# Second MLP's w_in operands at five steps a unit, and its first x operands in two halves

## The chip, the core and the metric

The kernel runs on one core of a Trainium2 chip. The metric is the device time of one execution in microseconds (us); smaller is better. Five engines work side by side, each through its own queue in order: PE (TensorE, matmuls), ACT (ScalarE), DVE (VectorE), POOL (GpSimd) and SP (SyncE, which here issues nearly all DMAs).

## What is computed

Linear attention, then an MLP with a squared ReLU, then an MLP with the Mish activation, all in float32. Cut to what matters:

```python
q_s = softmax(q, axis=-1);  k_s = softmax(k, axis=2)         # (4, 8, 576, 64) each
kv = np.einsum('bhsd,bhse->bhde', k_s, v)
x = np.einsum('bhsd,bhde->bhse', q_s, kv)                    # as (2304 tokens, 512)
h = x @ w_in;   y = (s * np.maximum(h, 0)**2 + b) @ w_out    # 512 -> 2048 -> 512
h = y @ w_in2;  g = h * np.tanh(softplus(h));  out = g @ w_out2
```

## The kernel before

A float32 product is made of three passes of matmuls over two float32r parts of each operand, high and low: `hi` is a cast on ACT, `lo` a subtraction on DVE (`split`, L177).

The first MLP runs in 80 steps: five chunks of tokens (512, 256, 512, 512, 512) by 16 slices f of d_ff. In step n PE does the 12 matmuls of h for step n + 2 (`LEAD`) and the 12 of y for step n; relu, square and `gh` on ACT and `gl` on DVE make y's operands from h. y is summed over the 16 steps of a chunk in four PSUM banks, one for each of the four m. In the last step of a chunk (15, 31, 47, 63, 79) `y_out` (L237) takes the banks out, two on ACT and two on DVE, into four tiles `ys`, and stores each to `y_dram`. The next chunk's y needs the banks.

Beside this the second MLP's weights are prepared in eight units for w_in and eight for w_out. A unit has four steps of work. `prep_load` (L255) makes four tiles, raw r0 and r1, t and s, and loads the raws. `prep_bits` (L262) writes t from the raws on ACT (L268) and DVE. `prep_sums` (L290) writes four sums of blocks of t into s, on DVE, and casts t into r0 and s into r1 on ACT. `prep_out` (L307) takes the casts off t and s and stores all four tiles to DRAM (`wi_d`, `wo_d`). `at(step, what, ...)` (L587) puts such work into a list for a step, and the main loop (L743) runs the lists: "prep" and "load" after `y_out`.

The tiles of a unit and the `ys` of `y_out` come from the same pool, "convert" (`cv`, L69), tag "t", four slots. From step 61 (`END`) on there is a second such pool, "convert2" (`cv2`), in the space that attention leaves. A tile has its slot from its first write until its last reader is done.

The order of an engine's instructions is not the program's alone. The framework lists them by a timeline of its own: what comes earlier in the program goes first, but an instruction further back goes ahead while those before it wait. So a load or a bit operation can run some steps before the step in which it is written.

At step 72 (`NS - 8`) the pool "second_x" opens, and `x_load` loads the first 768 tokens of y back as four tiles xf and adds a bias on ACT (L723); at step 74 `x_ops` makes from them the seven pairs of x operands `xo` in two halves j, with four tiles t1 to t4 each from a tag "c" with five slots (L735 to L741). At step 77 the pool "second_w" opens and the weights' ring starts to load. After step 79 the second MLP runs (`p` products on PE), with the seven products of a Strassen-like scheme.

The lines on which the prediction leans most:

```python
t1, t2, t3, t4 = (pools["x"].tile([P, HC], F32, tag="c", bufs=5, ...) for n in range(4))
tt(t1, b12, b11, ALU.subtract)
tt(t3, b22, b12, ALU.subtract)
tt(t2, b22, t1, ALU.subtract)
```

```python
        if f == NF - 1:
            y_out(n)
        run(n, "prep")
        run(n, "load")
```

Of the kernel before, what the change touches and what calls it, by code (L numbers as in the profile page):

```python
# [27 lines left out]
def kernel(  # L28
# [26 lines left out]
    NK = DM // P  # L55
# [13 lines left out]
    cv = ctx.enter_context(tc.tile_pool(name="convert", bufs=4))  # L69
# [43 lines left out]
    def load_raw(ph, z, f, part):  # L113
        src = srcs[ph, z].bitcast(I32)
        if z == "wi":
            nc.sync.dma_start(
                out=part.rearrange("p (k f) -> p k f", k=NK),
                in_=src[:, 2 * f * P:2 * (f + 1) * P].rearrange("(k p) f -> p k f", p=P),
            )
        else:  # L120
            nc.sync.dma_start(out=part, in_=src[f * P:(f + 1) * P, :])
# [55 lines left out]
    def split(hi, lo, src):  # L177
        nc.scalar.copy(out=hi, in_=src)  # L178
        minus(nc.vector, lo, src, hi)
# [27 lines left out]
    def emit_h(m, kks=None):  # L207
        ph, c, f = steps[m]
        if m not in h_ps:
            h_ps[m] = ps_h.tile([P, CM], F32, tag="h", name=f"h{m}")[:, 0:CHUNKS[c]]  # L210
        wh, wl = W[ph, "wi", f]
        for kk in kks or range(NK):
            o = slice(kk * P, (kk + 1) * P)
            passes(h_ps[m], (wh[:, o], wl[:, o]), x_t[ph, c, kk], kk == 0, kk == NK - 1)

    def emit_relu2(m):

        n = CHUNKS[steps[m][1]]
        hi = gp.tile([P, CM], F32R, tag="gh", name=f"gh{m}")[:, 0:n]
        lo = gp.tile([P, CM], F32R, tag="gl", name=f"gl{m}")[:, 0:n]  # L220
        r = rp.tile([P, CM], F32, tag="r", name=f"r{m}")[:, 0:n]
        nc.scalar.activation(out=r, in_=h_ps.pop(m), func=AF.Relu)  # L222
        nc.scalar.activation(out=r, in_=r, func=AF.Square)  # L223
        split(hi, lo, r)
        g_t[m] = (hi, lo)

    def emit_y(n):
        ph, c, f = steps[n]
        nt = CHUNKS[c]
        if f == 0:  # L230
            y_ps[c] = [ps_y.tile([P, DM], F32, tag=f"y{m}", name=f"y{m}_{n}") for m in range(NK)]
        wh, wl = W[ph, "wo", f]
        for m in range(NK):
            o = slice(m * P, (m + 1) * P)
            passes(y_ps[c][m][:, 0:nt], (wh[:, o], wl[:, o]), g_t[n], f == 0, f == NF - 1)

    def y_out(n):  # L237
        c = steps[n][1]
        nt = CHUNKS[c]
        for m, ps in enumerate(y_ps.pop(c)):  # L240
            ys = cv.tile([P, 2 * DM], F32, tag="t", name=f"ys{m}_{n}")[:, 0:nt]
            if m % 2:
                nc.vector.tensor_scalar(
                    out=ys, in0=ps[:, 0:nt], scalar1=sb_s, scalar2=None, op0=ALU.mult
                )
            else:
                nc.scalar.activation(out=ys, in_=ps[:, 0:nt], func=AF.Copy, scale=sb_s)
            nc.sync.dma_start(out=y_dram[c][:, m, :], in_=ys)
# [4 lines left out]
    prep = {}  # L253

    def prep_load(z, i, pool):  # L255
        r = [pool.tile([P, 2 * DM], I32, tag="t", name=f"r{j}_{z}{i}") for j in range(2)]
        for j in range(2):
            load_raw(1, z, i + j * NF // 2, r[j])
        t, s = (pool.tile([P, 2 * DM], F32, tag="t", name=f"{a}_{z}{i}") for a in "ts")
        prep[z, i] = (r, t, s)  # L260
# [26 lines left out]
    def tt(out, a, b, op):  # L287
        nc.vector.tensor_tensor(out=out, in0=a, in1=b, op=op)  # L288
# [298 lines left out]
    def at(slot, what, fn, *args):  # L587
        todo.setdefault((slot, what), []).append((fn, args))

    def run(slot, *what):  # L590
        for x in what:
            for fn, args in todo.pop((slot, x), ()):
                fn(*args)

    for c in range(1, NC):
        wide = CHUNKS[c - 1] == CM
        for hp in range(NP):
            s = (c - 1) * NF + 3 * hp - (c > 1)
# [24 lines left out]
    for i in range(NU):  # L623
        u, s = (0, i), i - 3
# [21 lines left out]
    END = (NC - 1) * NF - 3  # L646
    pools = {}
    for i in range(NF // 2):
        s = (17, 24, 31, 35, 39, 43, 47, 51)[i]
        at(s, "load", lambda i: prep_load("wi", i, cv), i)  # L650
        at(s + 1, "prep", prep_bits, "wi", i)
        at(s + 2, "prep", prep_sums, "wi", i)
        at(s + 3, "prep", prep_out, "wi", i)
        s = (55, 59, 62, 63, 66, 67, 70, 71)[i]
        at(s, "load", lambda i: prep_load("wo", i, pools["cv2"] if i in (2, 4, 6) else cv), i)
        at(s + 1, "prep", prep_bits, "wo", i)
        at(s + 2, "prep", prep_sums, "wo", i)
        at(s + 3, "prep", prep_out, "wo", i)
# [33 lines left out]
    def halves(t):  # L692

        n = t.shape[-1] // 2
        return t[:, 0:n], t[:, n:2 * n]
# [4 lines left out]
    def ring():  # L700
        return pools["ring"].tile([P, 2 * DM], F32R, tag="ring", name="ring")

    def wi_load(i):
        w = [ring() for _ in range(4)]
        for piece, t in enumerate(w):
            o = slice(HD if piece == 3 else 0, DM)
            nc.sync.dma_start(
                out=t.rearrange("p (n d) -> p n d", n=2)[:, :, o].bitcast(F32), in_=wi_d[i][:, piece, :, o]
            )
        return w  # L710

    xo = {}

    def x_load(sc):
        xf = []
        for kk in range(NK):
            t = pools["x"].tile([P, 2 * HC], F32, tag="s1", bufs=4, name=f"xf{sc}_{kk}")
            o = 0
            for c, a, b in PARTS[sc]:
                nc.sync.dma_start(out=t[:, o:o + b - a], in_=y_dram[c][:, kk, a:b])  # L720
                o += b - a

            nc.scalar.activation(out=t, in_=t, func=AF.Identity, bias=bsum[:, kk:kk + 1])  # L723
            xf.append(t)
        return xf

    def x_ops(sc, xf):
        for p in range(1, 8):
            xo[p] = halves(pools["x"].tile([P, 4 * HC], F32R, tag=f"xo{p}", name=f"xo{sc}_{p}"))

        for j in range(2):
            o = slice(j * HC, (j + 1) * HC)
            b11, b12 = xf[j][:, 0:HC], xf[j][:, HC:2 * HC]
            b21, b22 = xf[2 + j][:, 0:HC], xf[2 + j][:, HC:2 * HC]
            t1, t2, t3, t4 = (pools["x"].tile([P, HC], F32, tag="c", bufs=5, name=f"t{n}_{sc}") for n in range(4))  # L735
# [3 lines that stand above are left out]
            tt(t4, b21, t2, ALU.subtract)  # L739
            for p, b in ((1, b11), (2, b21), (6, t2), (5, t1), (7, t3), (3, b22), (4, t4)):  # L740
                split(xo[p][0][:, o], xo[p][1][:, o], b)  # L741

    for n in range(NS):  # L743
        ph, c, f = steps[n]
        if n == END:
            att.close()
            pools["cv2"] = ctx.enter_context(
                tc.tile_pool(name="convert2", bufs=4, side="right", reuse_waits="tile")
            )
        if n == NS - 8:  # L750
            wps[0][0].close()
            pools["x"] = ctx.enter_context(tc.tile_pool(name="second_x", bufs=1, side="right", reuse_waits="tile"))
            xf = x_load(0)
        if n == NS - 6:
            x_ops(0, xf)
        if n == NS - 3:
            wps[1][0].close()
            pools["ring"] = ctx.enter_context(tc.tile_pool(name="second_w", bufs=RING, side="right", reuse_waits="tile"))
            wi_next = {i: wi_load(i) for i in range(2)}
        m = n + LEAD  # L760
        boundary = m < NS and steps[m][2] == 0
        run(n, "att5", "att2", "att3")
        if n < NF:
            run(n, "abs", "hi", "lo", "bits")
        run(n, "att4_mm")
        if boundary:
            emit_y(n)
        if m < NS:
            emit_h(m)
            emit_relu2(m)  # L770
        run(n, "att5_mm", "att4", "att1", "sum")
        if not boundary:
            emit_y(n)
# [4 lines that stand above are left out]
        if m + 1 < NS and steps[m + 1][2] == 0:  # L778
            for kk in range(NK):
                x_split(0, steps[m + 1][1], kk)  # L780
# [24 lines left out]
    for sc in range(len(PARTS)):  # L805
# [43 lines left out]
        for p, src, j in ((1, None, 0), (2, g12, 2), (6, g11, 5), (7, g21, 6), (5, s1, 4), (3, g12, 3), (4, g22, 7)):  # L849
# [3 lines left out]
            for i in range(N2):  # L853
                if i % 2 == 0:
                    t = ring()
                    nc.sync.dma_start(out=t.bitcast(F32), in_=wo_d[i // 2][:, j].rearrange("p a b c -> p (a b c)"))
                    t = t.rearrange("p (a b c) -> p a b c", a=2, b=2)
# [33 lines left out]
            if p == 5 and sc + 1 < len(PARTS):  # L891
                xf = x_load(sc + 1)
            if p == 3 and sc + 1 < len(PARTS):
                x_ops(sc + 1, xf)
# [30 lines left out]
```

## Time and profile before

| | us |
|---|---|
| median of 3 runs | 859.76 (859.21 to 864.07) |
| the profiled execution | 859.61 |
| its span, first to last instruction | 857.8 |
| mean granted TensorE clock | 0.986 |

Rows of the profile give times from the span's start. A row of the timeline is: start, length, engine, line, operation, what it writes <- what it reads, shapes, how many were merged, and in brackets how long the engine was idle before it and what ended that. "SPq" is SP's queue, where DMAs are issued. `yd<-ys` are the stores of y_out, `r_wi` and `r_wo` the raw tiles of the units, `xf` the x tiles, `p` the second MLP's products. DMA rows give the time from issue to landing.

### The profile page before, as it was taken

Reading aid. Unit: us, or ns where it says so; the run is one execution under the profiler, and the core shown is the slowest. Engines: PE = TensorE matmul, PEld = TensorE weight load, DVE = VectorE, ACT = ScalarE, POOL = GpSimd, SP = SyncE. Lnnn points to the kernel's source line nnn. Section 1 sums busy time; section 2 is a strip of 40 time slices with the busy share of each in tenths; the row PEclk is TensorE's granted clock in tenths of the full one; section 3 lists DMA queues with packets and bytes.
Section 4 is the critical chain, followed back from the end, with each engine's and each line's share of the span. In section 5 each row is a group of like instructions: output and inputs, shape, how many; then the busy total and the mean of one; then the engine's idle time right before and its main releaser. Section 6 shows DMA issues by size and latency. Waiting matters only on the chain.

```text
span 857.8 us, 14201 instructions
## 1 busy us (share of the span) xinstructions
PE 823.6 (96%) x5060; PEld 739.4 (86%) x5060; DVE 630.1 (73%) x1190; ACT 496.6 (58%) x1109; POOL 3.7 (0%) x26
## 2 busy tenths in 40 slices
PE   5579999999899999999999899999999999999998
PEld 3357888998688888888888699999999999999998
DVE  5999866666766657778675867776877867778764
ACT  7676856578766756646655844455544447244542
POOL 1000000000000000000000000000000000000000
PEclk9679999999999999999999999999999999999999
DMA  8981331566465614455798497888887888878882
GB/s 232 304 300 45 123 89 41 151 189 175 141 209 159 210 60 139 169 174 189 263 319 275 136 367 248 267 269 278 300 278 249 275 257 307 290 250 270 257 266 78
DMA packets 130150, 184.44 MB, mean 215 GB/s; under 512 B 43552, under 2 KB 94240, under 8 KB 130080
## 3 DMA queue, kind: packets, MB, share of 16 engines
q1 hardware_dynamic: 128992, 182.49, 66.0%
q10 hardware_dynamic: 1088, 1.05, 0.4%
q8 instruction: 40, 0.66, 0.3%
q14 instruction: 30, 0.25, 0.1%
HBM read 140.51 MB, written 42.99 MB: 214 GB/s over the span
## 4 chain that ended last, share of the span: by engine, by line
PE 61%; DMA 13%; DVE 12%; ACT 6%; SPq 4%; issue 4%; DVEq 0%; ACTq 0%
PE p L185 39%; PE y L185 11%; PE h L185 9%; DMA r_wo<-in_moe_w_out_dram 4%; DMA raw<-in_moe_w_out_dram 2%; DMA q<-in_q_dram 2%; DMA yd<-ys 1%; DVE gl L175 1%; ACT q L449 1%; SPq L391 1%; DVE xo L175 1%; ACT r L222 1%; DMA r_wi<-in_moe_w_in_dram 1%; ACT r_wo L305 1%; DMA wi_d<-r_wi 1%
## 5 line engine op out<-in xcount | busy, mean ns | idle before, releaser
L185 PE MATMUL h<-xh,w 128*128 128x512 f32 (+1 forms) x640 | 201.1, 378 | 5.3 <-ACT w L164 3.2
L185 PE MATMUL y<-gh,w 128*128 128x512 f32 (+1 forms) x640 | 196.3, 371 | 2.6 <-ACT gh L178 2.6
L185 PE MATMUL p<-ring,op 128*128 128x256 f32 x1512 | 182.9, 283 | 0.1
L185 PEld LDWEIGHTS p<-ring,op 128*128 128x128 f32 x1512 | 182.4, 192 | 0.4 <-DVE op L175 0.3
L185 PE MATMUL p<-xo,ring 128*128 128x384 f32 x1008 | 175.9, 334 | 0.0
L185 PEld LDWEIGHTS p<-xo,ring 128*128 128x128 f32 x1008 | 174.6, 188 | 0.1
L185 PEld LDWEIGHTS h<-xh,w 128*128 128x128 f32 x640 | 118.6, 191 | 28.8 <-ACT xh L178 3.6
L185 PEld LDWEIGHTS y<-gh,w 128*128 128x128 f32 x640 | 117.2, 188 | 22.9 <-ACT gh L178 3.3
L185 PE MATMUL h<-xl,w 128*128 128x512 f32 (+1 forms) x320 | 120.2, 376 | 3.2 <-DVE xl L175 3.2
L185 PE MATMUL y<-gl,w 128*128 128x512 f32 (+1 forms) x320 | 119.0, 372 | 3.4 <-DVE gl L175 3.4
L817 ACT ACTIVATE g<-g 128x384 f32<-128x384 f32 x96 | 50.5, 526 | 111.2 <-DVE g L288 111.2
L178 ACT CAST op<-g 128x384 fp32r<-128x384 f32 x144 | 72.8, 512 | 46.5 <-PE p L185 45.7
L175 DVE TENSOR_TENSOR op<-g,op 128x384 fp32r<-128x384 f32 x144 | 78.9, 553 | 24.3 <-ACT op L178 24.1
L175 DVE TENSOR_TENSOR gl<-r,gh 128x512 fp32r<-128x512 f32 (+1 forms) x80 | 50.5, 632 | 49.2 <-ACT gh L178 49.0
L288 DVE TENSOR_TENSOR u<-u,p 128x384 f32<-128x384 f32 (+1 forms) x117 | 57.2, 499 | 29.5 <-PE p L185 29.0
L185 PEld LDWEIGHTS h<-xl,w 128*128 128x128 f32 x320 | 61.4, 192 | 14.2 <-DVE xl L175 4.4
L185 PEld LDWEIGHTS y<-gl,w 128*128 128x128 f32 x320 | 60.3, 188 | 14.9 <-DVE gl L175 5.2
L222 ACT ACTIVATE r<-h 128x512 f32<-128x512 f32 (+1 forms) x80 | 44.1, 551 | 45.8 <-PE h L185 27.2
L288 DVE TENSOR_TENSOR g<-u,p 128x384 f32<-128x384 f32 x96 | 53.1, 554 | 15.4 <-PE p L185 12.3
L449 ACT ACTIVATE q<-q,qm 128x64 f32<-128x64 f32 x144 | 48.1, 336 | 12.0 <-DVE qm L430 11.7
L223 ACT ACTIVATE r<-r 128x512 f32<-128x512 f32 (+1 forms) x80 | 47.1, 589 | 1.7
L178 ACT CAST gh<-r 128x512 fp32r<-128x512 f32 (+1 forms) x80 | 46.1, 577 | 1.7
(127 smaller groups left out, 824.2 us busy)
## 6 DMA issues: line engine op xcount, KB each, us to landing
ring<-wo_d SPq DMA_DIRECT2D x84, 512.0 KB, 4.6
ring<-wi_d SPq DMA_DIRECT2D x72, 512.0 KB, 4.8
raw<-in_moe_w_in_dram SPq DMA_DIRECT2D x16, 512.0 KB, 6.3
raw<-in_moe_w_out_dram SPq DMA_DIRECT2D x16, 512.0 KB, 7.5
r_wi<-in_moe_w_in_dram SPq DMA_DIRECT2D x16, 512.0 KB, 5.2
wi_d<-r_wi SPq DMA_DIRECT2D x16, 512.0 KB, 3.2
r_wo<-in_moe_w_out_dram SPq DMA_DIRECT2D x16, 512.0 KB, 5.9
wo_d<-r_wo SPq DMA_DIRECT2D x16, 512.0 KB, 3.0
```

The costliest lines, as they stand in the source:

```text
L175: eng.tensor_tensor(out=lo, in0=src, in1=hi.bitcast(F32), op=ALU.subtract)
L178: nc.scalar.copy(out=hi, in_=src)
L185: mm = nc.tensor.matmul(out=ps, lhsT=x, rhs=y, start=start, stop=stop)
L222: nc.scalar.activation(out=r, in_=h_ps.pop(m), func=AF.Relu)
L223: nc.scalar.activation(out=r, in_=r, func=AF.Square)
L288: nc.vector.tensor_tensor(out=out, in0=a, in1=b, op=op)
L305: nc.scalar.copy(out=a.bitcast(F32R), in_=src)
L391: nc.sync.dma_start(out=t[p0:p0 + n, h], in_=q[b, 2 * hp + h, s:s + n * rq, :].rearrange("(p r) d -> p r d", p=n),)
L449: nc.scalar.activation(out=t[:, i // rq, i % rq], in_=t[:, i // rq, i % rq], func=AF.Exp, bias=mx[:, i], accum_out=sm[:, i])
L817: nc.scalar.activation(out=t, in_=t, func=AF.Mish)
```

## The change

Units of w_in 3 to 7 start at steps 36, 41, 46, 51 and 56 in place of 35, 39, 43, 47 and 51, and the bits, sums and stores of every w_in unit come one step later after its load. w_out units start at 61, 62, 65, 66, 69, 70, 73 and 74 in place of 55, 59, 62, 63, 66, 67, 70 and 71, and the odd ones take the second pool, where units 2, 4 and 6 did. The first x tiles are loaded two at step 72 and two at step 74, and the x operands are made one half at step 74 and the other at step 77, just ahead of the ring's first loads. `x_load` and `x_ops` get arguments for that; the later calls use all.

```diff
     for i in range(NF // 2):
-        s = (17, 24, 31, 35, 39, 43, 47, 51)[i]
+        s = (17, 24, 31, 36, 41, 46, 51, 56)[i]
         at(s, "load", lambda i: prep_load("wi", i, cv), i)
-        at(s + 1, "prep", prep_bits, "wi", i)
-        at(s + 2, "prep", prep_sums, "wi", i)
-        at(s + 3, "prep", prep_out, "wi", i)
-        s = (55, 59, 62, 63, 66, 67, 70, 71)[i]
-        at(s, "load", lambda i: prep_load("wo", i, pools["cv2"] if i in (2, 4, 6) else cv), i)
+        at(s + 2, "prep", prep_bits, "wi", i)
+        at(s + 3, "prep", prep_sums, "wi", i)
+        at(s + 4, "prep", prep_out, "wi", i)
+        s = (61, 62, 65, 66, 69, 70, 73, 74)[i]
+        at(s, "load", lambda i: prep_load("wo", i, pools["cv2"] if i % 2 else cv), i)
         at(s + 1, "prep", prep_bits, "wo", i)
         at(s + 2, "prep", prep_sums, "wo", i)
         at(s + 3, "prep", prep_out, "wo", i)
...
-    def x_load(sc):
-        xf = []
-        for kk in range(NK):
+    def x_load(sc, kks=range(NK)):
+        xf = {}
+        for kk in kks:
...
-            xf.append(t)
+            xf[kk] = t
...
-    def x_ops(sc, xf):
-        for p in range(1, 8):
+    def x_ops(sc, xf, js=range(2)):
+        for p in range(1, 8) if 0 in js else ():
             xo[p] = halves(pools["x"].tile([P, 4 * HC], F32R, tag=f"xo{p}", name=f"xo{sc}_{p}"))
 
-        for j in range(2):
+        for j in js:
...
-            xf = x_load(0)
+            xf = x_load(0, (0, 2))
         if n == NS - 6:
-            x_ops(0, xf)
+            x_ops(0, xf, (0,))
+            xf = x_load(0, (1, 3))
         if n == NS - 3:
             wps[1][0].close()
             pools["ring"] = ctx.enter_context(tc.tile_pool(name="second_w", bufs=RING, side="right", reuse_waits="tile"))
+            x_ops(0, xf, (1,))
             wi_next = {i: wi_load(i) for i in range(2)}
```

## Rows read from the trace of the kernel before

**Rows 1.** The page, part 1: busy time, share of the span, instructions.

```profile
PE 823.6 (96%) x5060; PEld 739.4 (86%) x5060; DVE 630.1 (73%) x1190; ACT 496.6 (58%) x1109; POOL 3.7 (0%) x26
```

**Rows 2.** Windows: stretch, length, busy time by engine; last, tile t_wo alone (DVE, ACT).

```profile
core 0: us, PE busy (x) PEld busy (x) DVE busy (x) ACT busy (x) POOL busy (x), PEclk, DMA share, GB/s
50.00:58.00 8.00, 5.74 (x17) 4.00 (x18) 8.00 (x13) 6.24 (x8) 0.00 (x0) 0.79 1.05 388
212.00:232.00 20.00, 16.57 (x96) 12.39 (x97) 13.89 (x33) 14.44 (x40) 0.00 (x0) 1.00 0.51 151
410.00:440.00 30.00, 30.00 (x134) 24.83 (x133) 19.89 (x32) 16.74 (x27) 0.00 (x0) 1.00 0.82 279
440.00:462.00 22.00, 22.00 (x99) 18.22 (x98) 18.53 (x30) 13.61 (x21) 0.00 (x0) 1.00 0.85 283
462.00:474.00 12.00, 12.00 (x55) 9.93 (x54) 5.18 (x9) 7.02 (x12) 0.00 (x0) 1.00 0.81 273
474.00:490.00 16.00, 12.90 (x54) 9.46 (x53) 15.03 (x30) 13.04 (x25) 0.00 (x0) 1.00 0.37 123
...
361.00:492.00 131.00, 52.76 (x88) 18.91 (x24) 1.00 0.68 228
```

**Rows 3.** Timeline of PE: three places where y starts, one where it ends.

```profile
223.39 1.20 PE L185 MATMUL y<-gh,w 128*128 128x512 f32 x4 [1.49 <-ACT gh L178]
...
417.95 0.39 PE L185 MATMUL y<-gh,w 128*128 128x512 f32 x1
...
475.67 1.19 PE L185 MATMUL y<-gh,w 128*128 128x512 f32 x4 [1.12 <-ACT gh L178]
478.38 0.50 PE L185 MATMUL y<-gl,w 128*128 128x512 f32 x1 [1.51 <-DVE gl L175]
```

**Rows 4.** Timeline of SP's queue about steps 15, 43, 47, 58 and 63.

```profile
152.37 1.69 SPq L248 DMA_DIRECT2D yd<-ys  x3
154.83 0.38 SPq L116 DMA_DIRECT2D r_wi<-in_moe_w_in_dram  x1
...
298.12 0.36 SPq L316 DMA_DIRECT2D wi_d<-s_wi  x1
318.05 2.55 SPq L248 DMA_DIRECT2D yd<-ys  x4
320.69 1.02 SPq L116 DMA_DIRECT2D r_wi<-in_moe_w_in_dram  x2
...
380.75 0.79 SPq L121 DMA_DIRECT2D r_wo<-in_moe_w_out_dram  x1
...
412.66 0.61 SPq L121 DMA_DIRECT2D r_wo<-in_moe_w_out_dram  x1
413.36 4.17 SPq L248 DMA_DIRECT2D yd<-ys  x4
```

**Rows 5.** Timeline of DVE: the t tiles of x_ops, second half (one xo of the first).

```profile
477.17 0.55 DVE L288 TENSOR_TENSOR t<-xf 128x384 f32<-128x384 f32 x1
...
479.04 0.55 DVE L288 TENSOR_TENSOR t<-xf,xf 128x384 f32<-128x384 f32 x1
...
479.98 0.55 DVE L175 TENSOR_TENSOR xo<-t,xo 128x384 fp32r<-128x384 f32 x1
...
483.13 0.55 DVE L288 TENSOR_TENSOR t<-xf,t 128x384 f32<-128x384 f32 x1
```

**Rows 6.** The chain that ended last, in order of time: start, length, what.

```profile
322.51 1.36 PE y L185 x6
```

**Rows 7.** DMA issues in 317:321, then in 409:418: count, size, us to landing.

```profile
yd<-ys SPq DMA_DIRECT2D x4, 256.0 KB, 2.1
...
yd<-ys SPq DMA_DIRECT2D x4, 256.0 KB, 5.2
```

**Rows 8.** Timeline of ACT: unit 2's raw bits, and the first ys of step 63.

```profile
220.67 0.69 ACT L268 ACTIVATE t_wi<-r_wi 128x512 f32<-128x512 f32 x1 [2.44 <-DMA r_wi<-in_moe_w_in_dram]
...
410.10 0.68 ACT L247 ACTIVATE ys<-y,sb_s 128x512 f32<-128x512 f32 x1
```

## The prediction

> **What bounds the kernel now.** The page's first part comes first: PE is busy for 823.6 of 857.8 us [rows 1], so what the change can give back is idle PE time alone. The table by stretch says where that lies [rows 2]. After the start PE is busy in full, 30.00 us of 30 in 410:440 for one, except in two places: 16.57 of 20 us in 212:232 and 12.90 of 16 in 474:490. That is 3.4 + 3.1 = 6.5 us. PE's own timeline names the second place [rows 3]: there the y matmuls wait 1.12 us for gh from ACT and 1.51 us for gl from DVE, with DVE busy for 15.03 of those 16 us [rows 2], most of it x operands. The start, before step 17, holds nothing that the change touches. So preparing weights is off the path wherever it finds its tiles, and the change is to be judged by whom it makes wait.
>
> **How tiles are handed out.** The pool "convert" has four slots. A w_in unit takes all four (raw r0 and r1, t, s), and so does y_out, which empties the four y banks. SP's timeline shows that slots go in an order, not to whoever is ready [rows 4]. Unit 5's last store is issued at 298.12, yet unit 6's loads (step 47, behind y_out) come only at 320.69, after the stores of y_out of step 47 at 318.05; SP issues nothing in between. The same at 152.37 and 154.83. Is that the order of the tile() calls, or that in which tiles are first written? x_ops tells: it makes t1, t2, t3, t4 but writes t3 before t2, from a pool of five slots. In the second half t1 is written at 477.17, t3 at 479.04, t2 at 483.13 [rows 5]. The first half's t2 alone had been given back by 479.04, since the next copy of a t tile into xo is read at 479.98. So t3 took the only free slot past t2, which was made earlier: the order is that of the first write in the program. Everything below hangs on this reading.
>
> **The change, part by part.**
>
> w_in units 3 to 7 five steps apart, bits in the second step: the same instructions. They cost nothing by themselves, because they run ahead of their steps as tiles come free: unit 5's last store is written for step 46 and leaves at 298.12, 20 us before step 47's stores at 318.05 [rows 4]. A unit takes (380.75 - 320.69) / 3 = 20.0 us [rows 4], whatever step it is written for. Without that slack a step later would cost a step, 12 h and 12 y matmuls of 1.36 / 6 us [rows 6], 5.4 us; I take 0.
>
> What the spacing does change is unit 5. Its loads stand in step 46, its t in 48 and its s in 49, with y_out(47) between. By the order above it stops after its loads until y_out has its tiles, and y_out finds two free slots. Its third tile waits for the first store to land: 318.05 + 2.1 [rows 4, 7] = 320.2, evicted by 320.9 at 0.7 each [rows 8]; the fourth by 321.7. y(48) starts at 322.5 [rows 6], so this costs 0. In queue behind the late ys stand relu of the next steps on ACT and gl on DVE, about 1 us late, under a lead of two steps. What is late next is preparation: unit 5's bits at 323, then each unit in the place of the one after it, w_out unit 0 loading at 380.75 where unit 1 did.
>
> w_out unit 0 then meets y_out(63) in the same way, and worse: loads in 61, t in 62, sums in 63 but behind y_out. Its r0, r1 and t can't be given back, since they wait for sums that read t and fill s, and s stands behind the four ys. Four ys and s go through one slot. The first ys is done at 410.8 [rows 8]. Its store waits on SP behind loads and stores of the other pool, as now, until 413.4 [rows 4], and lands 5.2 us later under their traffic [rows 7], 418.6. The others find an idle queue (the next loads wait for this unit): 0.7 for a ys, 0.1 and 2.1 for a store. Second bank at 419.3, third 422.2, fourth 425.1. Now y(64) ends at 418.3 [rows 3]; its last three matmuls start 0.45 us before that row, at 417.5. PE can fill with the h of one step, 2.7 us, and 0.7 of the next y, so they are due by 421: cost 4.1 us. Ends: all stores at 2.1 and the first at once give 410.8 + 3 x 2.9 = 419.5, cost 0; all at 5.2 give 418.6 + 0.7 + 2 x 6.0 = 431.3, cost 10.3. I take 4.1, as the traffic of the first store is in the rows and that of the others is not. The ys also sit in ACT's and DVE's queues ahead of relu, gh and gl of steps 65 to 67.
>
> For such a store the Trainium skill (DMA: Bandwidth & Descriptors, Anatomy of one DMA, fitted there on the gpsimd path) has a fixed 2.0 us plus its bytes at 436 GB/s, by which 256 KB would take an estimated 2.6 us. The rows have 2.1 alone and 5.2 in traffic, so the fit misses the second. By it the fourth bank comes at about 421 and this part costs nothing, which makes the sum below 858.5.
>
> w_out spread over both pools: unit 1 moves from the first pool into the second, so one unit more is prepared after step 63. A unit is 52.76 / 8 = 6.6 us on DVE with t alone [rows 2]. DVE has 3.5 + 6.8 us free in 440:462 and 462:474 and 1 in 474:490. The first pool's last unit (6) follows unit 0's late end by two units and reaches the stretch of the x operands as unit 7 does now. I take +0.4; ends 0 (it fits the free DVE time) and +6.6 (all of it in front of gl). Unit 6's stores share SP with the ring's first loads and precede y_out(79)'s slots; the products' other four banks cover that.
>
> x operands in two halves: the same instructions, 22 of about 0.55 us on DVE [rows 5], the second half three steps later. It unties half of the knot in 474:490. PE lost 3.1 us there; I take 1.5 back, ends 3.1 and -2 (the second half meets the late unit and the first product, which needs both halves of xo1). The wait in 212:232 stays: units 0 to 2 load where they did, and y waits for gh [rows 3] while unit 2's raw bits hold ACT until their load lands [rows 8]. Ends -1 and +1.
>
> Sum against the profiled execution (859.61 us, span 857.8, 1.8 around it; the median of the runs is 859.76): 859.61 + 0 + 4.1 + 0.4 - 1.5 = 862.6, rounded to **862.5**.
>
> **Rivals.**
>
> A. *The order of slots doesn't bind* (it is that of the tile() calls, or the unit's t is written in time). For: w_in units do run steps ahead of their place. Against: rows 5. It decides at 318: if unit 5's t is written before y_out(47), the four parts leave 859.6 - 1.5 = 858, not slower. 855.5 to 860.5.
>
> B. *The end crowds.* The late first pool puts unit 6 and the second half of x between step 75 and the first product; DVE holds gl and xo1 for a unit, 6.6 us instead of 0.4, with 4.1 - 1.5 kept and part under PE's lead: 866, 863 to 870. Against: 10 us of free DVE time before 474.
>
> C. *The chain at y_out(63) runs at its slow end.* Each store lands in 5.2 us, the queues of ACT and DVE are held, cost 10.3: 859.6 + 10.3 - 1.5 + 0.4 = 868.8, and PE idles in stretches longer than any now. In 50:58, after a start with long waits, the granted clock was 0.79 [rows 2], between 1.2 and 2.4 GHz; (1 - 0.79) x 8 = 1.7 us for such a stretch, so 870.5, 868 to 876. The Trainium skill (TensorE: Matmul & The Clock Gate, the HAM clock gate) says that idle halves PE's clock until it is busy again; the rows of 212:232 and 474:490 show 1.00 across their waits of up to 1.5 us, and no longer wait is there to tell.
>
> D. *Both losses go.* Halves and later bits free gh and gl, slots don't bind: 859.6 - 6.5 = 853, 850.5 to 855. Against: what holds y at 223 is untouched in place.
>
> **How the numbers follow.** Forecast 0.50 (858 to 868.5), A 0.27, B 0.09, C 0.11, D 0.03. The time is that of the forecast. The range 856 to 870 leaves out D, the low end of A (0.05) and most of C (0.09): 0.17. About 1%, 8.6 us, is what a measurement can tell here. Over 868.4: 0.04 of the forecast's, 0.02 of B, 0.08 of C: 0.14. Under 851.2 only the far edge of D, 0.02; PE's idle time after the start is 6.5 us. Within: 0.84.
>
> **What would show it.** Step by step in the trace after: r_wi loaded near 280 but its t_wi not before 318; three units between 320 and 381 shifted by one; ys of step 63 some 3 us apart, each behind a landing yd, and PE's idle time near 418 to 425 with ys named. If t_wi of the unit loaded near 280 is written before 300, the reading of the order is wrong and A holds. In 474:490 PE's busy time should rise to about 14.4 of 16 us; if it falls, B. A granted clock under 1.00 after 410 is C.

## The result and the profile after

The changed kernel takes 869.75 us (median of 6 runs, 868.59 to 872.01); the kernel before took 861.24 in the same comparison (6 runs). The ratio is 1.011, 95% interval 1.0094 to 1.0126: slower by 1.1%. The profiled execution took 869.57 us (span 867.8) against 859.61 (857.8): 10.0 us more, where 2.9 were forecast.

The page's first part shows the same instructions with PE busy for 4.6 us more; its mean granted clock is 0.978 in place of 0.986 (busy, share, instructions; before in [rows 1]):

```profile
PE 828.2 (95%) x5060; PEld 742.6 (86%) x5060; DVE 630.8 (73%) x1190; ACT 496.5 (57%) x1109; POOL 3.7 (0%) x26
```

The table by stretch, in the columns of [rows 2], says where. From 410 to 474 PE is as busy as before, 410:440 with its late y_out(63) included. In 474:490 the same 54 matmuls take 13.77 us in place of 12.90, at a granted clock of 0.89, and PE waits that much less. Then 498:506 is nearly empty:

```profile
410.00:440.00 30.00, 30.00 (x134) 24.85 (x133) 19.33 (x31) 15.84 (x25) 0.00 (x0) 1.00 0.80 276
...
462.00:474.00 12.00, 12.00 (x55) 9.94 (x54) 11.40 (x20) 11.97 (x22) 0.00 (x0) 1.00 0.93 327
474.00:490.00 16.00, 13.77 (x54) 10.61 (x53) 11.69 (x22) 10.14 (x18) 0.00 (x0) 0.89 0.61 202
490.00:498.00 8.00, 7.84 (x35) 6.17 (x33) 5.33 (x11) 3.22 (x5) 0.00 (x0) 1.00 1.03 407
498.00:506.00 8.00, 1.27 (x4) 1.27 (x5) 3.69 (x5) 1.97 (x3) 0.00 (x0) 0.72 1.06 382
506.00:512.00 6.00, 6.00 (x30) 6.00 (x29) 2.65 (x5) 3.38 (x5) 0.00 (x0) 0.80 0.71 235
```

The timeline names the stall: the first product `p` of the second MLP and the four `ys` of the last y_out, whose idle time (in brackets) a store of a w_out unit ends each time.

```profile
503.99 0.69 ACT L247 ACTIVATE ys<-y,sb_s 128x512 f32<-128x512 f32 x1 [4.25 <-DMA wo_d<-r_wo]
504.73 10.45 PE L185 MATMUL p<-xo,ring 128*128 128x384 f32 x49 [6.89 <-ACT ys L247]
505.25 0.75 DVE L243 TENSOR_SCALAR ys<-y,sb_s 128x512 f32<-128x512 f32 x1 [4.16 <-DMA wo_d<-t_wo]
506.53 0.69 ACT L247 ACTIVATE ys<-y,sb_s 128x512 f32<-128x512 f32 x1 [1.85 <-DMA wo_d<-t_wo]
507.88 0.75 DVE L243 TENSOR_SCALAR ys<-y,sb_s 128x512 f32<-128x512 f32 x1 [1.88 <-DMA wo_d<-s_wo]
```

The same place in the kernel before: each ys waits for y's own last matmuls, and the product starts without a wait.

```profile
496.47 0.69 ACT L247 ACTIVATE ys<-y,sb_s 128x512 f32<-128x512 f32 x1 [3.17 <-PE y L185]
...
497.63 14.57 PE L185 MATMUL p<-xo,ring 128*128 128x384 f32 x83
```

Followed back in the chain of waits of after (start, length, what; 495 to 515), the first product waits for a ys, that for a store of 512 KB that is issued at 498.26 and lands 5.63 us later, and that for w_out unit 6's bits:

```profile
496.46 0.70 DVE t_wo L282
...
497.18 1.06 ACT r_wo L305
...
498.26 5.63 DMA wo_d<-r_wo
...
503.99 0.70 ACT ys L247
...
504.73 10.27 PE p L185 x48
```

Unit 6 holds all four slots of "convert" when y_out(79) needs them. The last of its stores is issued at 501.11. In the kernel before that pool's last unit (7) issued its last store at 487.05, 10 us ahead of y's end. In SP's queue of after, the last stores of units 0, 2, 4 and 6 (the first pool's) are 17 to 28 us apart:

```profile
432.25 1.43 SPq L318 DMA_DIRECT2D wo_d<-s_wo  x1
...
456.08 1.14 SPq L318 DMA_DIRECT2D wo_d<-s_wo  x1
...
483.95 0.48 SPq L318 DMA_DIRECT2D wo_d<-s_wo  x1
...
501.11 0.84 SPq L318 DMA_DIRECT2D wo_d<-s_wo  x1
```

The 10.0 us, added up: 6.89 of wait; a low clock behind it, since the 34 matmuls of 498:506 and 506:512 were busy 7.27 us and take 34 x 8.00 / 48 = 5.67 at full clock (48 products' matmuls took 8.00 us in the kernel before), 1.6; and three waits of products for `op` later, which the kernel before does not have, 0.8 (table of waits of PE after 512: engine and line, releaser, us in total, times, longest):

```profile
PE p L185 <- DVE op L175: 0.8, 3, 0.4
```

That is 9.3. Another 0.2 is there when the stall begins (y ends at 504.73 - 6.89 = 497.84, where the kernel before starts its first product at 497.63). The last 0.5 I did not trace.

### The profile page after: what moved, and what is told of

The parts are those of the page before. It is cut to its first block, busy times and chain, and to the rows that moved or that the text cites. A ratio compares the mean times of both kernels' runs of the same rounds, so it can differ in the third digit from the quotient of the medians.

```text
span 867.8 us, 14205 instructions
## 1 busy us (share of the span) xinstructions
PE 828.2 (95%) x5060; PEld 742.6 (86%) x5060; DVE 630.8 (73%) x1190; ACT 496.5 (57%) x1109; POOL 3.7 (0%) x26
## 4 chain that ended last, share of the span: by engine, by line
PE 68%; DMA 13%; DVE 10%; ACT 4%; SPq 3%; issue 2%; ACTq 0%; DVEq 0%
PE p L185 36%; PE y L185 15%; PE h L185 14%; DMA r_wo<-in_moe_w_out_dram 4%; DMA xf<-yd 2%; DMA raw<-in_moe_w_out_dram 2%; DMA wo_d<-r_wo 2%; DVE xo L175 1%; PE x L185 1%; DMA q<-in_q_dram 1%; ACT q L449 1%; DVE t L288 1%; DMA yd<-ys 1%; PE kv L484 1%; DVE op L175 1%
## 5 line engine op out<-in xcount | busy, mean ns | idle before, releaser
L185 PE MATMUL p<-xo,ring 128*128 128x384 f32 x1008 | 177.7, 336 | 6.9 <-ACT ys L247 6.9
```

Of the source, the lines that this page charges most:

```text
L185: mm = nc.tensor.matmul(out=ps, lhsT=x, rhs=y, start=start, stop=stop)
```

## Experiments

Three theories stood after that. The first: the loss is y_out(79) behind unit 6's slots, the wait of the first product for y's bank and the clock behind it. The second: the end as a whole is crowded (traffic, clock), and the wait stays or comes back elsewhere if the tiles are moved. The third: the x operands in halves set it. Each edit is against the kernel after unless it says otherwise.

**The last y_out in the second pool** (its four ys from "convert2"):

```diff
-            ys = cv.tile([P, 2 * DM], ...
+            ys = (pools["cv2"] if n == NS - 1 else cv).tile([P, 2 * DM], ...
```

> The changed kernel, with the four ys of step 79 taken from the second pool (free by then) and nothing else. Theory 1 (slots): the 6.9 us for which the first product waits is y_out(79) queued for slots of the first pool behind w_out unit 6; the products then start near 497.6 and the time falls by 7 us and the low clock's 2: 860 to 862. Theory 2 (crowding: one unit more and the x operands load DVE, ACT and DMA at the end): ys wait for their engines, or the products for something else; over 866.

Measured 858.46 us, ratio to before 0.9991 (0.9975 to 1.0008), below the 860 to 862 expected. The whole loss is gone, at one line's cost, though the units, the ring and the halves stay. Unit 6 is as late as ever (stores from 499.22), but nobody waits for it:

```profile
495.74 0.69 ACT L247 ACTIVATE ys<-y,sb_s 128x512 f32<-128x512 f32 x1 [1.92 <-PE y L185]
...
496.90 15.27 PE L185 MATMUL p<-xo,ring 128*128 128x384 f32 x87
```

The second theory falls.

**Unit 0 two steps earlier**, so that all its four tiles are first written ahead of y_out(63):

```diff
-        s = (61, 62, 65, 66, 69, 70, 73, 74)[i]
+        s = (59, 62, 65, 66, 69, 70, 73, 74)[i]
```

> The changed kernel, with w_out unit 0 starting at step 59 in place of 61, so that its sums (61) are written ahead of y_out(63) and its slots don't stay taken across it. Theory 1: y_out(63) finds free slots, unit 2 loads some 8 to 11 us earlier (431.3 now), units 4 and 6 follow, and y_out(79) waits 0 to 2 us: 861 to 864. Theory 2: the same work is at the end, 868 to 871.

Measured 861.46 us, 1.0013 (0.9997 to 1.0029), as expected. Unit 0's loads leave when they left in after (377.98 and 377.76), but its last store goes at 397.08 in place of 432.25, ahead of y_out(63). Unit 6's last store goes at 488.79 in place of 501.11, and the product starts at 498.15 without a wait. So the lateness came from unit 0 being caught across y_out(63), as the prediction said, but it was paid for some 80 us later.

**The x operands whole, as before:** loads at step 72, all operations at 74.

```diff
-            xf = x_load(0, (0, 2))
+            xf = x_load(0)
...
-            x_ops(0, xf, (0,))
-            xf = x_load(0, (1, 3))
+            x_ops(0, xf)
...
-            x_ops(0, xf, (1,))
```

> The changed kernel, with x loaded and made whole at steps 72 and 74 as before. Theory 1: unit 6 is still last in the first pool and late, 867 to 871. Theory 3 (the x operands in halves hold up unit 4's sums, and by it unit 6): unit 6 ends 5 us or more earlier, 861 to 865. The idle time of PE in 474:490 tells besides what the halves gave: by the prediction 1.5 us more idle here than in the changed kernel.

Measured 870.11 us, 1.0116 (1.0084 to 1.0148), as the first theory has it; the product's wait is 6.39 us. The third theory falls.

**w_in's steps and bits as before:**

```diff
-        s = (17, 24, 31, 36, 41, 46, 51, 56)[i]
+        s = (17, 24, 31, 35, 39, 43, 47, 51)[i]
...
-        at(s + 2, "prep", prep_bits, "wi", i)
+        at(s + 1, "prep", prep_bits, "wi", i)
...
```

> The changed kernel, with the w_in units at the steps of before, so that no unit straddles y_out(47). Theory 1 in its narrow form: unit 0 of w_out is held at y_out(63) whenever it was loaded, so 868 to 871 all the same. If it is the shift by one unit at step 47 that makes unit 6 late: 860 to 864.

Measured 873.65 us, 1.016 (1.0145 to 1.0175), outside both expectations. Undoing w_in's part brings nothing back; it costs 4 us more. The trace has the same stall with a later unit 6, whose first store lands at 507.9 in place of 503.9:

```profile
508.04 0.69 ACT L247 ACTIVATE ys<-y,sb_s 128x512 f32<-128x512 f32 x1 [2.06 <-DMA wo_d<-r_wo]
508.78 6.39 PE L185 MATMUL p<-xo,ring 128*128 128x384 f32 x24 [9.79 <-ACT ys L247]
```

SP's queue names the place: unit 6's second raw is issued at 490.71, in place of 484.53 in after, behind two loads of the ring and unit 4's last store:

```profile
488.19 1.16 SPq L707 DMA_DIRECT2D ring<-wi_d  x1
489.44 0.42 SPq L318 DMA_DIRECT2D wo_d<-s_wo  x1
489.92 0.70 SPq L707 DMA_DIRECT2D ring<-wi_d  x1
490.71 0.43 SPq L121 DMA_DIRECT2D r_wo<-in_moe_w_out_dram  x1
```

Unit 0 loads at 362.21 there, 15.6 us sooner than in after, and its last store still goes only at 434.06: it is held at y_out(63) however early it is loaded.

**w_out's steps and pools alone**, in the kernel before:

```diff
-        s = (55, 59, 62, 63, 66, 67, 70, 71)[i]
-        at(s, "load", lambda i: prep_load("wo", i, pools["cv2"] if i in (2, 4, 6) else cv), i)
+        s = (61, 62, 65, 66, 69, 70, 73, 74)[i]
+        at(s, "load", lambda i: prep_load("wo", i, pools["cv2"] if i % 2 else cv), i)
```

> The kernel before, with only the steps and the pools of the w_out units changed. If the new place of w_out's units in the two pools is all of the loss (unit 0's first three tiles ahead of y_out of step 63, its fourth behind it, unit 6 ahead of the last y_out in the same pool): 869 to 875 us, the first product waiting 6 to 10 us for y's first bank. If w_in's spacing or the halves have a part in it: 861 to 866.

Measured 872.55 us, 1.014 (1.012 to 1.0161), the product's wait 8.12 us. This part alone makes the whole loss, and some 3 us more (the two intervals of the ratio overlap). Its steps and its pools were not tried one without the other.

**w_in's bits in the second step alone**, in the kernel before (bits, sums and stores at s + 2, 3, 4):

> The kernel before, with bits, sums and stores of every w_in unit one step later and nothing else. Prediction and later theory alike: w_in units have some 20 us of slack on PE, so the time is that of before, 859 to 862 us. If w_in's later bits cost a step at any boundary of a chunk: 865 us.

Measured 859.44 us, 0.9988 (0.9973 to 1.0004): no cost, as forecast.

**The halves alone**, in the kernel before:

```diff
-            xf = x_load(0)
+            xf = x_load(0, (0, 2))
...
-            x_ops(0, xf)
+            x_ops(0, xf, (0,))
+            xf = x_load(0, (1, 3))
...
+            x_ops(0, xf, (1,))
```

> The kernel before, with the x operands in two halves and nothing else. The prediction: 1.5 us less, 858 us, with the y matmuls' waits of 1.1 and 1.5 us about 475 to 478 us halved. The rival: the framework puts the second half's operations right behind the first half's on DVE, although they are written three steps later, so the wait for gl stays and the time is 859.3 to 861.

Measured 861.06 us, 1.0012 (0.9998 to 1.0026): no gain. The halves do not come apart. DVE's timeline of the kernel after shows the first operation of the second half, written for step 77, 5.7 us behind the first of the first half and ahead of that half's last xo; gl, for which PE waits 1.67 us, stands behind 15 of the 22. With the halves alone the two are 4.8 us apart (473.19 and 477.94), and in the kernel before, where all is written for step 74, 6.4 (470.81 and 477.17). The waits of y in the run with the halves alone are 2.09 us for gh and 0.81 for gl, 2.9 as before 3.1, and the granted clock in 474:490 is 0.79. From the kernel after:

```profile
466.77 0.55 DVE L288 TENSOR_TENSOR t<-xf 128x384 f32<-128x384 f32 x1
...
472.46 0.55 DVE L288 TENSOR_TENSOR t<-xf 128x384 f32<-128x384 f32 x1
...
477.22 0.68 DVE L175 TENSOR_TENSOR gl<-r,gh 128x512 fp32r<-128x512 f32 x1
```

Nothing that the second half needs comes later than for the first: its y had been in DRAM since y_out(15) and y_out(31), and SP issues all eight loads of xf in one run from 458.02. That the framework therefore put it where DVE had room in its own timeline fits this; no run tests it.

**Both repairs at once** (unit 0 at 59, the last y_out in the second pool), to price the chain at y_out(63):

> The kernel after, with w_out unit 0 two steps earlier and the last y_out in the second pool. Beside the run that had the last y_out in the second pool alone (858.5 us) it takes away the chain of four ys through one slot at step 63. If that chain costs the 4.1 us of the prediction: 854 to 855.5. If it costs nothing, as PE's full 410:440 in the trace after says, or the 1.3 us of the trace with the last y_out moved: 857 to 859.

Measured 861.06 us, 1.0009 (0.9996 to 1.0021), above both expectations. Without the chain (the four ys are evicted from 409.2 to 412.0) the time is not lower than with it. So the chain costs nothing that can be measured; 4.1 us would have shown.

**y's banks in another place.** The prediction had four other banks cover a late y_out. The first edit put y's pool of banks behind those of h and attention:

```diff
-    ps_y = one.enter_context(tc.tile_pool(name="ps_y", bufs=1, ...
     ps_h = one.enter_context(tc.tile_pool(name="ps_h", bufs=2, ...
     ps_a = one.enter_context(tc.tile_pool(name="ps_a", bufs=2, ...
+    ps_y = one.enter_context(tc.tile_pool(name="ps_y", bufs=1, ...
```

> The kernel after, with the four banks of y placed behind those of h and of attention, so that the first products of the second MLP take banks that y does not hold. Nothing else is touched. The prediction's sentence that the products' other four banks cover a late last y_out is made true here. If the loss is the wait of the first product for y's first bank (6.89 us in the trace after) and the low clock behind it: the first product starts about 497.5 us, four products of 1.0 us each run, and the fifth waits for the first bank until about 504.7, some 3 us in place of 6.9: 864 to 867 us. If four banks did cover it: 859 to 861. If the first product waits for anything else: 869 to 870.5, as after.

Measured 871.8 us, 1.0134 (1.0116 to 1.0153): a miss. The first product no longer waits (497.26), but the second waits 9.50 us for the ys that DVE does last:

```profile
497.26 1.22 PE L185 MATMUL p<-xo,ring 128*128 128x384 f32 x6
...
507.18 0.75 DVE L243 TENSOR_SCALAR ys<-y,sb_s 128x512 f32<-128x512 f32 x1 [1.87 <-DMA wo_d<-s_wo]
507.99 7.21 PE L185 MATMUL p<-xo,ring 128*128 128x384 f32 x27 [9.50 <-DVE ys L243]
```

In all three programs (before, after and this one) the products take the banks in the order 0, 7, 6, 5, 4, 3, 1, 2, as the compiled program's list of banks has them. y holds 0 to 3 in after, so its first bank is the very first wanted, and 4 to 7 here. The next edit gave the products a fixed turn from bank 0 up, with y still in 4 to 7:

```diff
+    turn = list(range(8))
     def bank():
-        return ps2.tile([P, DM], F32, tag="p", bufs=8, name="p")
+        turn.append(turn.pop(0))
+        return ps2.tile([P, DM], F32, tag=f"p{turn[-1]}", bufs=1, name="p")
```

> The kernel after, with the eight banks of the second MLP's products taken in a fixed turn that begins with the four of h and of attention, and y's four behind them (the run before it, y_banks_last, had put y into other banks, but its second product took the bank that is emptied last). If the products' order of banks decides what a late last y_out costs: the first product starts about 497.4 us, four run in 1.0 us each (48 matmuls took 8.0 us in the kernel before), the fifth waits from 501.4 for the first ys, done about 504.7, and the next ones for the other ys up to 508.6; three to four products more are done by then than in after: 865 to 868 us. If what holds the first products is not the bank: 869 to 872 us.

Measured 867.43 us, 1.0077 (1.0053 to 1.0101), within the 865 to 868 expected. Four products (24 matmuls) run, the fifth waits 3.43 us, both 2 to 3 us later than expected:

```profile
499.64 4.36 PE L185 MATMUL p<-xo,ring 128*128 128x384 f32 x24
506.69 0.69 ACT L247 ACTIVATE ys<-y,sb_s 128x512 f32<-128x512 f32 x1 [3.44 <-DMA wo_d<-r_wo]
507.43 2.29 PE L185 MATMUL p<-xo,ring 128*128 128x384 f32 x6 [3.43 <-ACT ys L247]
```

So four free banks are worth four products, 4.36 us, where they are taken first, and here the first of y's banks was free only 4.36 + 3.43 = 7.8 us after the first product's start.

**GpSimd for the eight t operations** of the first x operands, with the last y_out in the second pool: a try at the wait for gl, for a version faster than both.

```diff
+    def tt_pool(out, a, b, op):
+        nc.gpsimd.tensor_tensor(out=out, in0=a, in1=b, op=op)
...
-            tt(t1, b12, b11, ALU.subtract)
+            (tt if sc else tt_pool)(t1, b12, b11, ALU.subtract)
```

(t2, t3 and t4 in the same way.)

> The kernel after, with the last y_out in the second pool and the eight t operations of the first x operands on GpSimd in place of DVE. If DVE's queue of x operands is what keeps gl (the wait of 1.81 us at 478.6 in the run with the last y_out moved): 4.4 us of operations leave DVE between 467 and 482, the wait falls to 0.5 or less, 856.5 to 858 us. If GpSimd's operations are slow or slow DVE's down, or the framework lists the rest as before: 858.5 to 861.

Measured 866.77 us, 1.007 (1.005 to 1.009), slower than both expectations and by 0.8% than the same kernel without it (0.9991). The wait for gl grew to 5.73 us, and the first product starts at 502.54 in place of 496.90. What the rows show of the reason is under the hardware, below. No version beat the kernel before; the best are level with it.

The runs side by side (stall: PE's wait ahead of its first products):

| kernel | stall, us | ended by | median, us | ratio to before |
|---|---|---|---|---|
| last y_out in second pool | 0 | | 858.46 | 0.9991 |
| both repairs | 0 | | 861.06 | 1.0009 |
| unit 0 two steps earlier | 0 | | 861.46 | 1.0013 |
| t on GpSimd, last y_out in second pool | 0 | | 866.77 | 1.0070 |
| four banks free | 3.43 + 0.36 | ys 1, ys 3 | 867.43 | 1.0077 |
| after | 6.89 | ys 1 | 869.75 | 1.0110 |
| x whole | 6.39 | ys 1 | 870.11 | 1.0116 |
| y's banks behind | 9.50 | ys 4 | 871.80 | 1.0134 |
| w_out alone | 8.12 | ys 1 | 872.55 | 1.0140 |
| w_in as before | 9.79 | ys 1 | 873.65 | 1.0160 |

The first three, 858.46 to 861.46, have intervals that overlap; their profiled executions differ by the clock in 474:490 (1.00, 0.89, 0.89), and whether that is the difference is open.

## Why the prediction was right or wrong

It forecast 862.5 us and no measurable change; the result is 869.75 and slower. The number lies inside the range, near its top, but that is luck: the top was held for a slow chain at y_out(63), and the loss is elsewhere. (The chances given for what lies outside add to 0.17, so that 0.83 and not 0.84 lay within.)

**PE's idle time decides: right.** All but 0.7 us of the loss is one stall, the low clock behind it and three small waits on PE.

**Slots go in the order of first writes: right.** What it said of unit 5 came so, though its loads left at 271.02 and not near 280. Its t, which tile() makes ahead of the ys of y_out(47), is written only after them; the late ys come at 320.17 and 320.96 (320.2 and about 321 forecast), and PE loses nothing there (busy for 45.00 of 45 us in 300:345):

```profile
320.17 0.69 ACT L247 ACTIVATE ys<-y,sb_s 128x512 f32<-128x512 f32 x1 [0.99 <-DMA yd<-ys]
320.96 0.75 DVE L243 TENSOR_SCALAR ys<-y,sb_s 128x512 f32<-128x512 f32 x1 [0.41 <-DMA yd<-ys]
...
323.24 1.19 ACT L268 ACTIVATE t_wi<-r_wi 128x512 f32<-128x512 f32 x2
```

**w_in's bits at nothing: right** (859.44 with the bits moved alone). The spacing was not run alone; in after PE has no idle time about step 47.

**The chain at y_out(63), 4.1 us: the chain right, its price wrong.** The banks come free at 417.5, 420.4 and 423.4, some 2 us ahead of the forecast:

```profile
416.77 0.74 DVE L243 TENSOR_SCALAR ys<-y,sb_s 128x512 f32<-128x512 f32 x1
419.71 0.69 ACT L247 ACTIVATE ys<-y,sb_s 128x512 f32<-128x512 f32 x1 [0.30 <-DMA yd<-ys]
422.69 0.75 DVE L243 TENSOR_SCALAR ys<-y,sb_s 128x512 f32<-128x512 f32 x1 [0.55 <-DMA yd<-ys]
```

The mis-sized term is "PE can fill with the h of one step, 2.7 us, and 0.7 of the next y", by which the fourth bank was due at 421. It came at 423.4 and PE never stopped. The matmuls of h alone in 412:424 (columns as above, without DVE and POOL) are 36 in after and 30 in before, six more that PE could take:

```profile
412.00:424.00 12.00, 8.46 (x36) 6.56 (x36) 1.20 (x2) 1.00 0.47 173
...
412.00:424.00 12.00, 7.21 (x30) 5.43 (x30) 1.18 (x2) 1.00 0.97 337
```

And seven matmuls of y, not three, start from 422.02 on the three free banks for step 65. In after PE is busy 30.00 of 30 us in 410:440; in two other runs whose edits touch later work alone (the last y_out moved, four banks free) it is 28.65 and 28.91, with waits for gh at 430.86 and 431.80. So the price is 0 to 1.4 us.

**One more w_out unit after step 63, +0.4: the step that failed.** What it priced at 0.4 us is nearly the whole loss, 6.89 us of wait and 1.6 of low clock behind it. Two of its sentences failed. "The first pool's last unit (6) follows unit 0's late end by two units and reaches the stretch of the x operands as unit 7 does now": units 2 and 4 do stand between, but unit 6's last store goes at 501.11, not as unit 7's at 487.05. I counted DVE's free time and not the time that a unit takes in a pool with slots for one alone. The prediction had that time, 20.0 us: three units behind 432.25 end at 492.3, 5 us behind unit 7 and still 5 us ahead of y's end. Units 2, 4 and 6 took 24, 28 and 17 us by the stores above. What the chain of waits of after shows of that is a crowded end: unit 4's last operations stand among the x operands on DVE, and unit 6's second raw lands 7.48 us after its issue, with nine loads of the ring issued from 487.00 on.

```profile
474.07 2.42 DVE xo L175 x5
...
482.79 1.13 DVE s_wo L288
483.92 0.48 DVE xo L175
...
484.53 7.48 DMA r_wo<-in_moe_w_out_dram
```

How much each of these adds no run tells apart. The second sentence, "Unit 6's stores share SP with the ring's first loads and precede y_out(79)'s slots; the products' other four banks cover that", saw the wait and covered it with banks whose order was not known. The first product takes the bank that y gives back first, so nothing was covered.

**The halves, -1.5 us: wrong, 0.** The prediction used the rule that the framework pulls work forward for w_in's units, and not for these operations, to which it applies as well. PE's busy time in 474:490 rose to 13.77 us, where 14.4 was the sign, but for the same 54 matmuls: its waits fell by 0.9 us and the low clock took 0.9.

**The rivals.** A (slots do not bind) is refuted. B had the place, unit 6 at the end, but its mechanism (DVE holding gl and xo1) is not the one: the product waits for a bank, and DVE's x operands only add to unit 4's lateness. C had the clock, but at 418; its sign, a granted clock under 1.00 after 410, was there for other waits, in 474:490 and at the stall.

## What to carry to other kernels

A pool that serves two kinds of work in one order lets the late end of one become the late start of the other: follow the chain of a pool's users, unit by unit, to the last one before a boundary, and see who stands behind it. Giving the consumer on the path its own slots (here one line) brought back the whole loss, and so did moving the one producer that was caught; the rest of the change could stay. Before a late release is called covered by other buffers, find out which buffer is wanted first.

## What the runs showed of the hardware

**PE's clock after short waits.** y waits for gh or gl about 474 to 483 in all 13 profiled executions, and in eight of them the granted clock in 474:490 is under 1.00. It stayed 1.00 with waits of 1.12 and 1.51 us [rows 3] (before), 1.81 alone, 1.74 alone, 1.41 alone, and 0.92 and 1.79. It was 0.89 with 0.56 and 1.67 (after), 0.82 and 1.80, 0.34 and 1.63, 1.80 alone, 0.49 and 2.03, and 2.66; it was 0.79 with 2.09 and 0.81, and with 1.78 and 5.73 (GpSimd for t). The length of the wait does not tell them apart: 1.81 is among the first and 1.63 among the second. In after the clock stood at 0.50, the lower of the two levels (1.2 and 2.4 GHz), from 478 to 481, right behind the wait of 1.67 us. That cost 0.9 us, as the stretch's 54 matmuls show (13.77 us against 12.90). After the stall of 9.50 us (the run with y's banks behind) it stood at 0.50 for all of 506:512:

```profile
506.00:512.00 6.00, 4.01 (x13) 4.02 (x14) 1.30 (x2) 3.18 (x5) 0.00 (x0) 0.50 0.54 175
```

The Trainium skill (TensorE: Matmul & The Clock Gate, Part 1: The HAM clock gate) has the clock at half or full rate by how busy PE has been recently. The trace agrees as to the two rates: 0.50 here, and 1.00 again in 520:600, with PE busy for 80.00 of 80 us.

**GpSimd beside DVE.** A t operation of 128x384 took 0.55 us on DVE and 1.1 to 1.8 on GpSimd. DVE's operations beside it went from 0.55 to 1.37 us, and a pair of those on t_wo from 1.29 (in after) to 2.81. Between two GpSimd operations, from 472.00 to 474.42, DVE is back at 0.55:

```profile
465.07 1.36 POOL L291 TENSOR_TENSOR t<-xf 128x384 f32<-128x384 f32 x1 [460.19 <-DMA xf<-yd]
...
465.59 2.81 DVE L277 SCALAR_TENSOR_TENSOR t_wo<-r_wo,t_wo 128x512 int32<-128x512 int32 x2
468.33 1.37 DVE L175 TENSOR_TENSOR xo<-xf,xo 128x384 fp32r<-128x384 f32 x1
...
472.47 0.55 DVE L175 TENSOR_TENSOR xo<-xf,xo 128x384 fp32r<-128x384 f32 x1
```

The Trainium skill (GPSIMD Engine Reference, Specifications) says that GpSimd shares its SBUF interfaces with DVE and contends with DVE instructions of two SBUF inputs; both of these have two, and the trace agrees.
